# In a fused attention and feed-forward kernel: a cast of g moved from VectorE to ScalarE in batch index 1, sums of the weight forms put behind g's remainder, P's blocks in pairs

## The chip, the cores and the metric

The kernel runs on one core of one Trainium2 chip. The metric is the device time of one execution in microseconds, given as the median of several runs. Five units matter here: PE (TensorE, which runs the matmuls), ACT (ScalarE), DVE (VectorE), and the queues of SP (SyncE) with the DMA engines behind it, which load and store. PE, DVE and ACT each take their instructions strictly in the order in which the program has them, so an instruction that waits holds up whatever stands behind it on its engine.

## The reference: what is computed

Attention through 32 memories a head, then a feed-forward layer. Eight batch indices b, 8 heads, 576 positions, head size 64; model width 512, inner width 2048. Cut to what matters:

```python
a = softmax(phi, axis=2)                    # over the 576 positions
k_m = einsum('bhsm,bhsd->bhmd', a, k)       # 32 memories a head
v_m = einsum('bhsm,bhsd->bhmd', a, v)
scores = matmul(q, k_m.T) / 8
attn = softmax(scores, axis=-1)             # over the 32 memories
x = matmul(attn, v_m)                       # laid out as (4608, 512)
h = x @ w_in                                # (512, 2048)
g = h * sigmoid(h)
out = g @ w_out                             # (2048, 512)
```

All in float32. The matmuls get there by splitting an operand into a high part of fewer bits and the remainder, each in the type fp32r, and adding up three products (high x high, high x low, low x high).

## The kernel before

**The fold.** x is never formed. For each batch index the kernel makes P = v_m x w_in on PE (`p_mm`, matmuls at L646, in blocks of 512 columns called P(b,0) to P(b,3)), splits it into high and low parts (`pm`: an ACT copy at L674, a DVE subtraction at L676), and the first feed-forward product is then h = attn x P, 256 memories deep instead of 512.

**Slots.** The main loop runs over b = 0..7 and, in each, over 16 slots. In a slot of b = 0 or 1, PE makes one block of h (L698, 12 matmuls of 128x288 into the PSUM bank pair `h`), ACT takes SiLU of the 512 main tokens into `gbuf` (L725) and of the 64 tokens left over into `gleft` (L727), and `split` makes g's high part ghi (L715, a DVE cast) and its remainder glo = g - ghi (L717, DVE). PE then runs the second product of the slot *before* it (`acc`, L743, 12 matmuls of 128x512, of which every third reads glo). So in PE's queue a slot reads: h(s), then the events of the slot, then acc(s-1). There is one `h` buffer: h(s+1) starts when L725 and L727 of slot s have read h. From b = 2 on, the second product has another shape (L851 for h, L865 to L881 for g's parts, L890 for 21 matmuls of `sum`), in the manner of Strassen, with fewer multiplications; it needs sums and differences of blocks of w_out, the *forms*. After the 16 slots of an odd b come four *left steps*, in which the tokens left over of two batch indices go through the second product (`accleft`, L743 in b = 1; `lsum`, L974, in b = 3, 5, 7).

**The forms** are prepared once, in the slots of b = 1, by `w_forms(j, step)`, j = 0..7. Step 0 is on DVE: a sum of w_out's high and low parts (L811, 128x1024), then four additions of 128x256 (L815 to L818). Step 1 splits the four results into high parts (L832, on ACT, `t` and `kept`) and remainders (L833, DVE). For even j both steps stand in one slot (2, 5, 8, 11), for odd j step 1 follows one slot after step 0.

**The next batch's attention** is spread over the slots in small steps, which a table of events sets: `ev(b, slot, function, ...)`. They are the maximum of phi (`phi_max`), its folding over the partitions (`phi_fold`), the subtraction, the exponential (`phi_exp`, L319 on ACT, in slot 3 of b = 1), the product with k and v (`e_mm`, L335, slot 5), the turning of its result (`e_tr`, L367 on PE and L368/L369 behind it, slot 9), the scores (`s_all`, L382, slot 10), their softmax (`s_max` L426, `s_sub` L430, `s_exp` L434, `s_sum` L438, `s_norm` L444), turned back as attn's parts, and P's blocks. Exponential and SiLU need different tables of ACT's, so `phi_exp` and `s_exp` each stand between two table loads.

**What sets the order.** PE's order is that of the code. ACT's is too, from b = 1 on. On DVE and SP the framework sorts the instructions by its own estimates, unless `behind(i, other)` adds an edge, so that i is placed after other. `run` and the loop of b = 1 call the functions; `last_split` holds the instructions that made g's remainders so far. e_tr, s_all and e_mm write their results into columns of the `h` banks that L698 leaves free, and wait for L727 (L867 from b = 2 on) of the same slot, which reads there.

## Time and profile before

| | |
|---|---|
| median of 3 runs | 678.95 us (678.32 to 679.55) |
| the profiled execution | 678.81 us, of which its span 677.0 us |
| PE, share of the span busy | 99% |
| DVE | 77% |
| ACT | 55% |
| b = 1, from 106.54 to 197.58 us | 91.04 us: PE 90.94, DVE 76.13, ACT 39.48 us busy |
| b = 2, from 197.58 to 268.95 us | 71.37 us: PE 71.06, DVE 54.23, ACT 39.46 us busy |

A row of the timeline has the start in us, the duration in us, the engine, the line, the operation, what it writes and reads, the shape and how many instructions the row holds; in brackets the idle time ahead of it and who ended it. PE's matmuls are pipelined, so the modelled durations of neighbours overlap: the distance from start to start is what a step costs PE. A regular slot of b = 1 shows as the distance from one h row to the next.

### The profile page before, as it was taken

To read this page: it belongs to the slowest core of one execution; us is meant where nothing else is said; L and a number is where in the kernel's file an instruction comes from. 1 tells how busy PE (TensorE), PEld (TensorE's weight loads), DVE (VectorE), ACT (ScalarE), POOL (GpSimd) and SP (SyncE) were. 2 spreads that over 40 slices of the span, in tenths; PEclk is the share of its full clock that TensorE was granted. 3 is DMA by queue.
4 is the path that set the end of the run, shared out by engine and by line. 5 is a ranking of instruction groups with operands and counts; after the bars stand their busy time and mean duration, and the time that the engine had idled before them with its cause. 6 is when DMAs were issued, how large, how long until landed. Compare 5 with 4: busy or idle time off the path is not lost.

```text
span 677.0 us, 14546 instructions
## 1 busy us (share of the span) xinstructions
PE 667.3 (99%) x5794; PEld 588.6 (87%) x5794; DVE 518.2 (77%) x1092; ACT 369.1 (55%) x682; POOL 0.7 (0%) x6
## 2 busy tenths in 40 slices
PE   8999999999999999999999999999999999999997
PEld 3578778787888998999988999899997999889996
DVE  4897899888948689868877678877877668867653
ACT  3878684533625556654655546564654546554541
POOL 0000000000000000000000000000000000000000
PEclk9999999999999999999999999999999999999999
DMA  9988984224270552253520535216430304300001
GB/s 338 374 321 295 307 312 174 93 106 147 80 233 21 185 176 106 79 189 111 178 98 16 185 95 178 72 40 239 156 127 32 86 2 156 106 35 17 32 1 47
DMA packets 37907, 93.92 MB, mean 139 GB/s; under 512 B 4688, under 2 KB 21456, under 8 KB 34256
## 3 DMA queue, kind: packets, MB, share of 16 engines
q1 hardware_dynamic: 36816, 90.22, 38.5%
q10 hardware_dynamic: 1024, 2.77, 1.1%
q8 instruction: 46, 0.75, 0.5%
q14 instruction: 21, 0.17, 0.1%
HBM read 77.22 MB, written 15.73 MB: 137 GB/s over the span
## 4 chain that ended last, share of the span: by engine, by line
PE 85%; DVE 4%; ACT 2%; issue 2%; DMA 1%; SPq 0%; DVEq 0%; ACTq 0%
PE sum L890 34%; PE h L851 21%; PE acc L743 10%; PE h L698 5%; PE lsum L974 5%; PE bg L646 4%; PE accleft L743 2%; DMA q<-in_q 1%; PE bg L335 1%; PE h L335 1%; PE bg L382 1%; PE pacc L646 1%; ACT raw L174 0%; ACT aparts L879 0%; DVE win L178 0%
## 5 line engine op out<-in xcount | busy, mean ns | idle before, releaser
L851 PE MATMUL h<-aparts,pm 128*128 128x288 f32 x1152 | 168.7, 295 | 0.0
L851 PEld LDWEIGHTS h<-aparts,pm 128*128 128x128 f32 x1152 | 157.4, 188 | 0.8
L865 ACT ACTIVATE gbuf<-h 128x512 f32<-128x512 f32 x96 | 57.3, 597 | 117.0 <-PE h L851 113.7
L890 PE MATMUL sum<-wo_hi,aparts 128*128 128x256 f32 x384 | 102.6, 289 | 0.0
L890 PE MATMUL sum<-kept,aparts 128*128 128x256 f32 x576 | 100.1, 282 | 0.0
L890 PE MATMUL sum<-wo_lo,aparts 128*128 128x256 f32 x384 | 100.0, 282 | 0.0
L870 DVE TENSOR_TENSOR gbuf<-gbuf 128x256 f32<-128x256 f32 x96 | 40.6, 423 | 71.4 <-ACT gbuf L865 70.9
L879 ACT ACTIVATE aparts<-gbuf 128x512 fp32r<-128x512 f32 x86 | 54.4, 633 | 63.5 <-DVE gbuf L874 63.5
L743 PE MATMUL acc<-wo_hi,gparts 128*128 128x512 f32 x256 | 85.0, 397 | 0.1
L890 PEld LDWEIGHTS sum<-wo_hi,aparts 128*128 128x128 f32 x384 | 72.7, 189 | 11.5 <-ACT gleft L867 10.1
L890 PEld LDWEIGHTS sum<-kept,aparts 128*128 128x128 f32 x576 | 82.6, 191 | 0.0
L881 DVE TENSOR_TENSOR gparts<-gbuf,aparts 128x512 fp32r<-128x512 f32 x86 | 59.6, 693 | 19.6 <-ACT aparts L879 19.6
L890 PE MATMUL sum<-wo_hi,gparts 128*128 128x256 f32 x384 | 73.2, 281 | 0.0
L890 PEld LDWEIGHTS sum<-wo_lo,aparts 128*128 128x128 f32 x384 | 73.1, 190 | 0.0
L890 PE MATMUL sum<-kept,gparts 128*128 128x256 f32 x288 | 65.5, 282 | 0.0
L743 PEld LDWEIGHTS acc<-wo_hi,gparts 128*128 128x128 f32 x256 | 47.6, 188 | 14.0 <-DVE t L833 1.7
L890 PEld LDWEIGHTS sum<-wo_hi,gparts 128*128 128x128 f32 x384 | 59.4, 190 | 0.0
L698 PEld LDWEIGHTS h<-aparts,pm 128*128 128x128 f32 x372 | 51.8, 188 | 6.3 <-issue 2.3
L698 PE MATMUL h<-aparts,pm 128*128 128x288 f32 x372 | 56.0, 299 | 0.4 <-ACT aparts L611 0.4
L869 ACT ACTIVATE aparts<-gbuf 128x384 fp32r<-128x384 f32 x96 | 50.4, 525 | 0.0
L743 PE MATMUL acc<-wo_lo,gparts 128*128 128x512 f32 x128 | 49.4, 393 | 0.3 <-DVE wo_lo L182 0.2
L890 PEld LDWEIGHTS sum<-kept,gparts 128*128 128x128 f32 x288 | 47.9, 190 | 0.0
(225 smaller groups left out, 955.9 us busy)
## 6 DMA issues: line engine op xcount, KB each, us to landing
win<-win_saved SPq DMA_DIRECT2D x24, 1024.0 KB, 4.9
kv<-in_kv SPq DMA_DIRECT2D x28, 516.0 KB, 4.9
q<-in_q SPq DMA_DIRECT2D x16, 576.0 KB, 6.3
raw<-in_w_in SPq DMA_DIRECT2D x14, 512.0 KB, 7.3
raw<-in_w_out SPq DMA_DIRECT2D x6, 1024.0 KB, 7.2
win_saved<-win SPq DMA_DIRECT2D x4, 1024.0 KB, 8.6
phi<-in_phi SPq DMA_DIRECT2D x7, 576.0 KB, 8.4
out<-oo SPq DMA_DIRECT2D x26, 128.0 KB, 2.1
```

Of the source, the lines that this page charges most:

```text
L335: nc.tensor.matmul(pt[p][M * r : M * (r + 1), :KVW], e[:, p, c, M * r : M * (r + 1)], kvt[c][:, p, r], start=c == 0, stop=False, skip_grou ...
L646: nc.tensor.matmul((bg[p][M * r : M * (r + 1)] if beside else bg[M * r : M * (r + 1), p, :w]).rearrange("p (k f) -> p k f", f=P), kvT[D * ...
L698: nc.tensor.matmul(h[:, hf, :HALF], wt[:, p, fs], a[:, p, hf * HALF : (hf + 1) * HALF], start=n[hf] == 0, stop=n[hf] == 5, skip_group_chec ...
L743: nc.tensor.matmul(acc[key], gt[:, cs], wt[:, fc], start=fc == 0 and n == 0, stop=fc == NFC - 1 and n == 2)
L851: nc.tensor.matmul(h[:, i, :HALF], wt[:, p, f : f + P], a[:, p], start=n == 0, stop=n == 5)
L865: nc.scalar.activation(gbuf[:, :MAIN].rearrange("p (i f) -> p i f", i=2), h[:, :, :w], AF.Silu)
L869: nc.scalar.activation(hi[:, :3], g[:, 1:4], AF.Copy)
L870: nc.vector.tensor_tensor(g[:, 4:6], g[:, :1].broadcast_to([P, 2, P]), g[:, 1:3], op=ALU.subtract)
L879: nc.scalar.activation(hi[:, 3:], g[:, 4:], AF.Copy)
L881: last_split.append(nc.vector.tensor_tensor(lo[:, 3:], g[:, 4:], hi[:, 3:], op=ALU.subtract))
L890: nc.tensor.matmul(sums[bank][:, place * Q : (place + 1) * Q], gt[:, k], wt, start=bank not in begun, stop=True, skip_group_check=True,)
L974: nc.tensor.matmul(sums[k], part[gt][:, 2 * i + k], wt[:, fc], start=n == 0 and i == 0 and m == 0, stop=True, skip_group_check=True,)
```

## The change

- **g's high part.** In b = 1 (and in the last slot of b = 0) ghi is made by an ACT copy (L713), which comes right behind L727 in ACT's queue, and not by the DVE cast L715.
- **The forms' first sum.** L811 of every j is now placed behind g's remainder (L717) of the slot in which it is called; before, this held for j = 0 alone.
- **P's blocks two by two.** P(2,0) and P(2,1) stood in slots 12 and 14 of b = 1, each alone; now both stand at the third left step of b = 1, interleaved, the second one in a free pair of `acc` banks. P(2,2) and P(2,3) stood in slots 1 and 2 of b = 2; now both stand in slot 0. P(3,0) and P(3,1) go from slots 13 and 14 of b = 2 to 12 and 14. The last quarter of the saved w_in that P(2,3) needs is loaded at the first left step of b = 1, where it was loaded in slot 0 of b = 2.
- **The attention steps of b = 2.** e_tr goes from slot 8 to 7, s_all from 9 to 8, s_max from 10 to 9. The maximum of phi for batch index 4 goes in halves, in slots 10 and 13; it was whole in slot 14.

Lines behind L811 have a number smaller by one in the changed kernel (L832 is L831, L833 is L832 there).

```diff
             i = nc.vector.tensor_tensor(f, as_f32(wo_hi[:, c]), as_f32(wo_lo[:, c]), op=ALU.add)
-            if j == 0:
-                behind(i.ins, last_split[-1])
+            behind(i.ins, last_split[-1])
...
-        ev(b, ex + 4, e_tr, n)
-        ev(b, ex + 5, s_all, n)
-        ev(b, 9 if early else 10, s_max, n, ALL)
+        ev(b, ex + 4 - (not early), e_tr, n)
+        ev(b, ex + 5 - (not early), s_all, n)
+        ev(b, 9, s_max, n, ALL)
...
-            ev(b, NFC + 2 if b % 2 else 13 + k, p_mm, n, k * JW, JW, True, b % 2 and k)
+            ev(b, NFC + 2 if b % 2 else (13 if early else 12 + k) + k, p_mm, n, k * JW, JW, True, b % 2 and k)
...
-            ev(b, 7 if early else 14, phi_max, m)
+            for p in range(2):
+                ev(b, 7 if early else 10 + 3 * p, phi_max, m, (0, 1) if early else (p,))
+                if early:
+                    break
...
-            pair = b > 2 and b % 2 == 0
+            pair = b % 2 == 0
             if not pair:
                 ev(b, 0, win_load, b, 3)
-            ev(b, 0 if b > 2 else 1, p_mm, b, 2 * JW, JW)
+            ev(b, 0, p_mm, b, 2 * JW, JW)
...
-            for k in range(3):
-                ev(b, 12 if k == 2 else 6 + k, win_load, n, k)
+            for k, slot in enumerate((6, 7, 12, NFC)):
+                ev(b, slot, win_load, n, k)
             for k in range(2):
-                ev(b, 12 + 2 * k, p_mm, n, k * JW, JW)
+                ev(b, NFC + 2, p_mm, n, k * JW, JW, True, k)
...
-            gs = split(silu(b, fc, h))
+            gs = split(silu(b, fc, h), steps=(2, 1) if b or fc == NFC - 1 else (0, 1))
...
-                if b > 1:
-                    run(b, NFC + n)
+                run(b, NFC + n)
```

**DVE, slots 8 and 9 of b = 1.** `wf` is the workspace of one j of the forms (j = 4 here, then j = 5 from the last row of before), `gparts` holds ghi and glo, `t_1605` and `kept` take the forms' parts, kvT is e_tr's result. Before:

```order
L811 TENSOR_TENSOR wf<-wo_hi,wo_lo 128x1024
L815 TENSOR_TENSOR wf<-wf 128x256
L816 TENSOR_TENSOR wf<-wf 128x256
L715 CAST gparts<-gbuf 128x512
L817 TENSOR_TENSOR wf<-wf 128x256
L717 TENSOR_TENSOR gparts<-gbuf,gparts 128x512
L818 TENSOR_TENSOR wf<-wf 128x256
L833 TENSOR_TENSOR t_1605<-wf,t_1605 128x256
L833 TENSOR_TENSOR kept<-wf,kept 128x2x256
L833 TENSOR_TENSOR kept<-wf,kept 128x256
L811 TENSOR_TENSOR wf<-wo_hi,wo_lo 128x1024
```

The same place of the changed kernel:

```order
L717 TENSOR_TENSOR gparts<-gbuf,gparts 128x512
L811 TENSOR_TENSOR wf<-wo_hi,wo_lo 128x1024
L814 TENSOR_TENSOR wf<-wf 128x256
L815 TENSOR_TENSOR wf<-wf 128x256
L832 TENSOR_TENSOR t_1605<-wf,t_1605 128x256
L816 TENSOR_TENSOR wf<-wf 128x256
L817 TENSOR_TENSOR wf<-wf 128x256
L832 TENSOR_TENSOR kept<-wf,kept 128x2x256
L832 TENSOR_TENSOR kept<-wf,kept 128x256
L368 COPY kvT_1654<-h 128x128
L717 TENSOR_TENSOR gparts<-gbuf,gparts 128x512
```

Slot 8's remainder (L717) stood behind the sum L811 and three of the four additions; now it stands ahead of all five, and the cast L715 is gone. The next slot's remainder now stands behind e_tr's copy L368, where the next sum L811 stood ahead of that copy and of the remainder.

**ACT, slots 11 to 13 of b = 1.** `t_1776` and `kept` are the forms' high parts of j = 6, `gbuf` and `gleft` the SiLUs of slots 12 and 13, `sc` the scores, of which L434 takes the exponential, `pm<-bg` the high part of P(2,0). Before:

```order
L832 ACTIVATE t_1776<-wf 128x256
L832 ACTIVATE kept<-wf 128x2x256
L832 ACTIVATE kept<-wf 128x256
L725 ACTIVATE gbuf<-h 128x512
L727 ACTIVATE gleft<-h 128x64
L434 ACT_TABLE_LOAD
L434 ACTIVATE sc_1703<-sc_1703 128x1152
L674 ACTIVATE pm<-bg 128x1024
L725 ACT_TABLE_LOAD
L725 ACTIVATE gbuf<-h 128x512
L727 ACTIVATE gleft<-h 128x64
```

The same place of the changed kernel:

```order
L831 ACTIVATE t_1776<-wf 128x256
L831 ACTIVATE kept<-wf 128x2x256
L831 ACTIVATE kept<-wf 128x256
L725 ACTIVATE gbuf<-h 128x512
L727 ACTIVATE gleft<-h 128x64
L713 ACTIVATE gparts<-gbuf 128x512
L434 ACT_TABLE_LOAD
L434 ACTIVATE sc_1703<-sc_1703 128x1152
L725 ACT_TABLE_LOAD
L725 ACTIVATE gbuf<-h 128x512
L727 ACTIVATE gleft<-h 128x64
```

The copy of g's high part L713 has come between slot 12's SiLU and the table load for the exponential, and the copy of P(2,0) has left its place ahead of the load back.

## The prediction

> **What bounds the kernel now.** The page comes first, its row of busy shares:

> ```profile
> PE 667.3 (99%) x5794; PEld 588.6 (87%) x5794; DVE 518.2 (77%) x1092; ACT 369.1 (55%) x682; POOL 0.7 (0%) x6
> ```

> PE is busy for 667.3 us of the span of 677.0, so only two things can move the time: what PE itself has to do, and the few places where it waits. A gain must be PE work left out or one of those waits ended; a loss is a new wait. The windows by batch index show where there is room beside PE (columns: length, then busy us of PE, PEld, DVE, ACT):

> ```profile
> 106.54:197.58 91.04, 90.94 (x644) 73.92 (x642) 76.13 (x149) 39.48 (x75) 0.00 (x0) 1.00 0.41 144
> ```

> In b = 1, where the change is, DVE is busy 84% and ACT 43% of the stage. That is a mean; PE waits or not by what stands in one queue at one moment. So I went on to the timeline of each engine, slot by slot. PE's, in b = 1:

> ```profile
> 125.21 1.76 PE L698 MATMUL h<-aparts,pm 128*128 128x288 f32 x12
> ...
> 127.53 0.73 PE L743 MATMUL acc<-wo_hi,gparts 128*128 128x512 f32 x2
> ...
> 129.94 1.75 PE L698 MATMUL h<-aparts,pm 128*128 128x288 f32 x12
> ...
> 153.59 0.44 PE L367 MATMUL h<-ident,kvn 128*128 128x128 f32 x2
> ...
> 158.31 1.09 PE L382 MATMUL bg<-q,kvT 64*32 64x288 f32 x32
> 159.24 0.35 PE L382 MATMUL h<-q,kvT 64*32 64x64 f32 x16
> ...
> 162.38 1.75 PE L698 MATMUL h<-aparts,pm 128*128 128x288 f32 x12
> ...
> 166.71 1.75 PE L698 MATMUL h<-aparts,pm 128*128 128x288 f32 x12
> ...
> 172.28 1.75 PE L698 MATMUL h<-aparts,pm 128*128 128x288 f32 x12
> ...
> 176.61 1.75 PE L698 MATMUL h<-aparts,pm 128*128 128x288 f32 x12
> ```

> From h row to h row an undisturbed slot takes 166.71 - 162.38 = 4.33 us. The slot with P(2,0) in it takes 172.28 - 166.71 = 5.57, so one block of P alone costs 1.24. The slot that begins at 125.21 takes 4.73, which is 0.40 too long.

> **The change part by part: gains.** First the pairs. The chain of waits has the four left steps of b = 1 without and of b = 3 with a pair of P's blocks:

> ```profile
> 189.57 8.17 PE accleft L743 x36
> ...
> 347.81 2.75 PE lsum L974 x12
> ...
> 352.43 5.67 PE lsum L974 x24
> ```

> 36 matmuls of a left step take 8.17 us; with a pair between them they reach from 347.81 to 352.43 + 5.67 = 358.10, which is 10.29. A pair costs 2.12, two blocks apart 2 x 1.24 = 2.48: a gain of 0.36. There are two new pairs (left step of b = 1, slot 0 of b = 2), and I price both by this row: **-0.72**.

> Second, the wait behind 125.21. On DVE:

> ```profile
> 125.66 1.22 DVE L811 TENSOR_TENSOR wf<-wo_hi,wo_lo 128x1024 f32<-128x1024 f32 x1
> 126.80 0.68 DVE L717 TENSOR_TENSOR gparts<-gbuf,gparts 128x512 fp32r<-128x512 f32 x1
> ...
> 137.38 0.35 DVE L361 TENSOR_SCALAR kvn<-h,rs 128x128 f32<-128x128 f32 x1 [0.43 <-ACT kvn L359]
> ...
> 147.05 1.22 DVE L811 TENSOR_TENSOR wf<-wo_hi,wo_lo 128x1024 f32<-128x1024 f32 x1
> ...
> 167.21 1.35 DVE L430 TENSOR_TENSOR sc<-sc,smx 128x1152 f32<-128x1152 f32 x1
> ```

> The forms' sum went ahead of the slot's remainder, which ended at 127.48; PE's matmul that reads it began at 127.53. With the sum behind the remainder this goes: **-0.40**.

> Third, b = 2, in PE's timeline:

> ```profile
> 241.47 1.09 PE L382 MATMUL bg<-q,kvT 64*32 64x288 f32 x32
> 242.75 0.35 PE L382 MATMUL h<-q,kvT 64*32 64x64 f32 x16 [0.18 <-ACT gleft L867]
> ...
> 249.72 1.76 PE L851 MATMUL h<-aparts,pm 128*128 128x288 f32 x12
> ...
> 253.83 1.76 PE L851 MATMUL h<-aparts,pm 128*128 128x288 f32 x12
> ...
> 258.05 1.87 PE L851 MATMUL h<-aparts,pm 128*128 128x288 f32 x12
> ...
> 263.47 1.76 PE L851 MATMUL h<-aparts,pm 128*128 128x288 f32 x12
> ...
> 268.98 1.77 PE L851 MATMUL h<-aparts,pm 128*128 128x288 f32 x12
> ```

> The second part of s_all comes 1.28 after the first here, and 159.24 - 158.31 = 0.93 in b = 1: 0.35 of waiting for gleft. The slots from 253.83 take 4.22, 5.42 and 5.51, against 4.11 ahead of them and 4.11 + 1.24 = 5.35 with a block: 0.11 + 0.07 + 0.16 = 0.34. All of these steps are respaced; I take both waits to go, **-0.69** (0 to -0.69, since respaced steps can meet other ones). Gains in all: 0.72 + 0.40 + 0.69 = **1.81**.

> **Losses.** They come from ACT's queue, which in b = 1 keeps the order of the code. ACT's timeline, and the group that prices the new copy:

> ```profile
> 118.33 0.60 ACT L725 ACTIVATE gbuf<-h 128x512 f32<-128x512 f32 x1 [3.45 <-PE h L698]
> ...
> 124.32 0.58 ACT L725 ACTIVATE gbuf<-h 128x512 f32<-128x512 f32 x1
> ...
> 128.81 0.60 ACT L725 ACTIVATE gbuf<-h 128x512 f32<-128x512 f32 x1
> 129.30 0.22 ACT L727 ACTIVATE gleft<-h 128x64 f32<-128x64 f32 x1
> ...
> 148.39 0.60 ACT L725 ACTIVATE gbuf<-h 128x512 f32<-128x512 f32 x1 [2.57 <-issue]
> ...
> 152.67 0.60 ACT L725 ACTIVATE gbuf<-h 128x512 f32<-128x512 f32 x1 [0.90 <-PE h L698]
> ...
> 164.22 0.60 ACT L725 ACTIVATE gbuf<-h 128x512 f32<-128x512 f32 x1 [3.90 <-PE h L698]
> ...
> 170.25 0.21 ACT L727 ACTIVATE gleft<-h 128x64 f32<-128x64 f32 x1
> 170.48 1.28 ACT L434 ACT_TABLE_LOAD   x1
> ...
> 175.40 0.60 ACT L725 ACTIVATE gbuf<-h 128x512 f32<-128x512 f32 x1
> ```

> ```profile
> L879 ACT ACTIVATE aparts<-gbuf 128x512 fp32r<-128x512 f32 x86 | 54.4, 633 | 63.5 <-DVE gbuf L874 63.5
> ```

> The same copy, 128x512 to fp32r, takes 0.63 us here. Back to back I count 0.55, since a SiLU of 0.60 is followed 0.49 later (128.81 to 129.30). A SiLU and its small one take 0.49 + 0.22 = 0.71. In most slots ACT waits for h and the copy is free. It isn't free where ACT's queue runs without a gap into the next SiLU; there are three such places.

> *Slots 3 to 5.* The window over this one slot shows ACT full, 4.69 of 4.73 us:

> ```profile
> 125.21:129.94 4.73, 4.63 (x25) 3.77 (x25) 4.38 (x10) 4.69 (x7) 0.00 (x0) 1.00 0.00 0
> ```

> It holds table load, exponential, load and the SiLU of slot 4 without a gap. Put in ahead of the first load, the copy moves that SiLU to 129.36 and its end to 130.07. h of slot 5 could start at 125.21 + 4.33 = 129.54. **+0.55**, which takes back the 0.40 just gained. Then h of slot 6 waits for L361 (at 137.38), which reads e_mm's result out of h and now has more of the forms ahead of it on DVE: between 0 and 0.4, I take **+0.2**.

> *Slot 9.* The sum of j = 4 ran at 147.05, in DVE's gap ahead of slot 8's split. Now it waits for the remainder, which waits for the copy, which waits for the SiLU at 148.39. Behind it come four additions, then `kept` on ACT, and `kept` stands ahead of slot 9's SiLU. How long that chain is shows where a sum already stood behind its split (j = 0, slot 2): 124.32 - 118.33 = 5.99 from SiLU to SiLU. The copy on ACT, longer than the cast, adds 0.1, so slot 9's SiLU comes at 148.39 + 6.09 = 154.48 in place of 152.67, and both SiLUs end at 155.19. The e_tr of slot 9 follows that in PE's queue and waits for it; it ran at 153.59. **+1.6** (1.0 if `kept` finds a gap, 2.2 if DVE is late besides). All of PE's later work queues behind it.

> *Slots 11 to 13* (times as before, since this whole stretch shifts together). j = 6 has the same chain: from slot 11's SiLU at 164.22 to slot 12's 6.09, and 0.3 more as s_sub (1.35, at 167.21) now stands ahead of the remainder and is not quite hidden: 170.6, end 171.3. h of slot 13 could start at 166.71 + 4.33 = 171.04 now that P(2,0) is gone: 0.3. Then copy, load, exponential, load: from the load at 170.48 to the SiLU at 175.40 it took 4.92, of which about 1.25 belonged to P(2,0)'s copy and its wait. So slot 13's SiLU comes at 171.3 + 0.55 + 3.67 = 175.5, its end at 176.25, and h of slot 14 then. Without waits it would be 171.04 + 4.33 = 175.37: **+0.9** in all (0 to 1.2). Put otherwise: the P block that left this slot leaves a hole, and ACT fills it.

> [...]

> The rest I price at nothing, the loads too:

> ```profile
> win<-win_saved SPq DMA_DIRECT2D x24, 1024.0 KB, 4.9
> ```

> A quarter of w_in lands 4.9 us after its issue. The last one is issued at the first left step now, and the left steps take 8.17 + 2.12 until slot 0 of b = 2 needs it; if it were late by the rest of its time, PE would wait there for about that rest. If the first half of phi's maximum, at slot 10 of b = 2, had to wait for its workspace, the DVE work queued behind it would be late, and PE for that; the third rival prices it.

> Losses: 0.55 + 0.2 + 1.6 + 0.9 = **3.25**. Net 3.25 - 1.81 = +1.44, on the profiled execution's 678.81: 680.25, said as **680.2**. That execution lies 0.14 under the median of the runs, so the basis needs no correction.

> **The rivals.**

> *ACT has room, and only the gains stay.* The windows speak for it: ACT 39.48 of 91.04, DVE 76.13; taking sixteen casts off the fuller engine should shorten the chains that end in `kept`, and slot 2, where the sum stood behind the split before, cost PE nothing. It decides if slot 9's SiLU still ends ahead of 153.59, and slots 4 and 13 likewise: then all four losses vanish, 678.81 - 1.81 = **677.0**. Against it: the chain of 6 us was measured, with a slot of 4.33. [...]

> *Half of it.* Slot 9 and slot 4 lose as worked out, but slots 6 and 11 to 13 catch up, since PE's longer wait at slot 9 also lets DVE clear its queue: 0.55 + 1.6 - 1.81 = +0.34, **679.1**.

> *DVE blocks in b = 2.* The half maximum at slot 10 waits for its workspace, and the respaced steps meet others: the 0.69 is not gained, three slots more come late by 0.16 each as the one at 263.47 does (0.5), and h of slot 6 takes the upper 0.4: 1.44 + 0.69 + 0.5 + 0.2 = +2.83, **681.6**.

> That the change does not do what it says is ruled out by the order of the instructions, which shows each move.

> **How the numbers follow.** A difference of 0.2%, 1.36 us, is about what a measurement of this kernel can tell from no change. My forecast (+1.44) gets 0.50; with its terms' bounds it is above 1.36 in somewhat over half of that, 0.30, and within in 0.20. Half of it: 0.24 (0.20 within, 0.03 slower, 0.01 faster). Only gains: 0.15 (0.12 faster, 0.03 within). Blocked b = 2: 0.11, slower. Together faster 0.13, same 0.43, slower 0.44. The range leaves out the most of the rival with gains alone and a tail above: from 678.2, half a microsecond and more under the 679.1 of the halfway case, to 681.8, above the worst case's 681.6.

> **What the changed profile would show.** Slot 9 of b = 1: SiLU (L725) about 6.1 after slot 8's, L367 with PE idle over 1 us ahead of it and gleft L727 as the releaser. Slots 3 to 5: h rows 4.9 apart, not 4.33. Slots 12 to 14: two h rows that are 4.6 and 5.0 apart. The left steps of b = 1 longer by 2.1, slots 12 and 14 without L646. In b = 2, 0.9 between the two rows of s_all. It is wrong if L367 follows L646 without a gap, or if PE's idle time in b = 1 does not grow.

## The result, and the profile after

The changed kernel takes **684.07 us** (median of 6 runs, 682.77 to 685.5), the kernel before 678.74 (6 runs, 678.32 to 679.55): ratio 1.0076, 95% interval 1.0065 to 1.0087. It is slower, by 5.3 us. The direction was forecast; the size was forecast as 1.4, and the time lies outside the range of 678.2 to 681.8.

The page of the changed kernel, busy shares and the row of the granted clock in 40 slices:

```profile
PE 668.4 (98%) x5794; PEld 590.0 (86%) x5794; DVE 513.3 (75%) x1079; ACT 378.0 (55%) x701; POOL 0.7 (0%) x6
PEclk9999999999999999899999999999999999999999
```

PE's busy time grew by 1.1 us only, the span by 5.3: most of the loss is waiting. And one slice, the seventeenth (from 273 to 290 us), has a clock below full, which the profiled execution of the kernel before does not have anywhere. First PE's timeline in b = 1, where the prediction put its losses:

```profile
105.84 1.85 PE L698 MATMUL h<-aparts,pm 128*128 128x288 f32 x12
...
124.52 1.80 PE L698 MATMUL h<-aparts,pm 128*128 128x288 f32 x12
...
129.51 1.85 PE L698 MATMUL h<-aparts,pm 128*128 128x288 f32 x12 [0.46 <-ACT gleft L727]
...
137.89 1.86 PE L698 MATMUL h<-aparts,pm 128*128 128x288 f32 x12 [0.28 <-DVE kvn L361]
...
155.36 0.44 PE L367 MATMUL h<-ident,kvn 128*128 128x128 f32 x2 [1.60 <-ACT gleft L727]
...
168.41 1.75 PE L698 MATMUL h<-aparts,pm 128*128 128x288 f32 x12
173.24 1.87 PE L698 MATMUL h<-aparts,pm 128*128 128x288 f32 x12 [0.34 <-ACT gleft L727]
178.29 1.86 PE L698 MATMUL h<-aparts,pm 128*128 128x288 f32 x12 [0.44 <-ACT gleft L727]
182.73 1.75 PE L698 MATMUL h<-aparts,pm 128*128 128x288 f32 x12
```

Every new wait in b = 1 stands where it was forecast, with the releaser that was forecast: the h rows of slots 5, 6, 13 and 14, and L367 in slot 9. ACT's timeline has the two chains behind them:

```profile
124.32 0.64 ACT L713 ACTIVATE gparts<-gbuf 128x512 fp32r<-128x512 f32 x1
124.97 1.28 ACT L319 ACT_TABLE_LOAD   x1
...
148.45 0.60 ACT L725 ACTIVATE gbuf<-h 128x512 f32<-128x512 f32 x1 [2.03 <-PE h L698]
...
154.62 0.58 ACT L725 ACTIVATE gbuf<-h 128x512 f32<-128x512 f32 x1
```

The copy stands ahead of the table load and takes 0.65 from start to start there; from slot 8's SiLU to slot 9's it is 6.17, where 6.09 was worked out. In b = 2 the steps run without the waits of before:

```profile
239.48 1.09 PE L382 MATMUL bg<-q,kvT 64*32 64x288 f32 x32
240.41 0.35 PE L382 MATMUL h<-q,kvT 64*32 64x64 f32 x16
...
255.59 1.76 PE L850 MATMUL h<-aparts,pm 128*128 128x288 f32 x12
...
260.91 1.76 PE L850 MATMUL h<-aparts,pm 128*128 128x288 f32 x12
...
265.00 1.76 PE L850 MATMUL h<-aparts,pm 128*128 128x288 f32 x12
...
270.31 1.77 PE L850 MATMUL h<-aparts,pm 128*128 128x288 f32 x12
```

The two parts of s_all are 0.93 apart, and slots 12 to 14 take 5.32, 4.09 and 5.31. At the last slot of b = 2 the changed kernel is 270.31 - 268.98 = 1.33 us late. That this is close to the forecast of 1.44 is partly luck. In this execution b = 1 began at 105.84, 0.70 earlier than the 106.54 of before; the prediction has no term ahead of b = 1, and the 0.70 is there already at the h row of 86.36 (before 87.06), up to which both kernels run the same instructions. Counted from the start of b = 1, the loss up to here is 2.03. The other 4 us are lost in the next few microseconds, at a place of which the prediction does not speak: slot 1 of b = 3. PE there, in the changed kernel, with the window behind the wait (length, busy us of PE, PEld, DVE, ACT, POOL, then the granted clock):

```profile
279.73 1.75 PE L850 MATMUL h<-aparts,pm 128*128 128x288 f32 x12
...
284.15 0.39 PE L889 MATMUL sum<-wo_hi,aparts 128*128 128x256 f32 x1 [1.97 <-DVE x L930]
...
287.36 2.27 PE L850 MATMUL h<-aparts,pm 128*128 128x288 f32 x12
```

```profile
284.10:289.40 5.30, 5.20 (x27) 5.00 (x28) 4.52 (x11) 0.63 (x1) 0.00 (x0) 0.68 0.15 49
```

```profile
285.08:288.50 3.42, 3.42 (x16) 3.42 (x17) 3.13 (x8) 0.63 (x1) 0.00 (x0) 0.50 0.23 77
```

From h row to h row it is 7.63 us. PE waits 1.97 for L930, which reads the sums of b = 2 out of PSUM. The 0.68 of the window of 5.30 us is a mean: for 3.42 us of it the granted clock is 0.50, ahead of that and behind it 1.00. In the kernel before the same slot takes 4.07:

```profile
278.40 1.75 PE L851 MATMUL h<-aparts,pm 128*128 128x288 f32 x12
...
282.47 1.74 PE L851 MATMUL h<-aparts,pm 128*128 128x288 f32 x12
```

Why L930 came late, DVE's timeline and SP's queue show. Before:

```profile
279.34 0.41 DVE L931 TENSOR_TENSOR x<-sum,oo 128x256 f32<-128x256 f32 x1
...
281.11 0.29 DVE L303 COPY wide<-fm 128x256 f32<-128x256 f32 x1
```

```profile
270.78 0.32 SPq L88 DMA_DIRECT2D win<-win_saved  x1
272.51 2.48 SPq L88 DMA_DIRECT2D qz<-qm  x4
278.12 1.82 SPq L88 DMA_DIRECT2D fm<-fm  x3
```

After:

```profile
282.81 0.29 DVE L303 COPY wide<-fm 128x256 f32<-128x256 f32 x1 [1.73 <-DMA fm<-fm]
283.02 0.42 DVE L930 TENSOR_TENSOR x<-sum,oo 128x256 f32<-128x256 f32 x1
```

```profile
273.32 2.48 SPq L88 DMA_DIRECT2D qz<-qm  x4
275.90 0.53 SPq L88 DMA_DIRECT2D win<-win_saved  x1
277.29 1.77 SPq L88 DMA_DIRECT2D fm<-fm  x3
```

Two orders have turned round. On DVE, L303 (the last step of folding phi's maximum for batch index 4, which waits for the small moves `fm`) now stands *ahead* of L930, and PE waits for L930. On SP, the 1 MB load of w_in's last quarter now stands *between* the fold's two moves. The DMA issues of the stretch from 270 to 290 us give the landing time of the second move, changed kernel first, then before:

```profile
fm<-fm SPq DMA_DIRECT2D x3, 1.0 KB, 4.7
```

```profile
fm<-fm SPq DMA_DIRECT2D x3, 1.0 KB, 1.8
```

A move of 1 KB issued behind a load of 1 MB took 4.7 us in place of 1.8. Why the move takes longer behind the load, no run shows.

### The profile page after: what moved, and what is told of

The parts are those of the page before. It is cut to its first block, busy times and chain, and to the rows that moved or that the text cites. A ratio compares the mean times of both kernels' runs of the same rounds, so it can differ in the third digit from the quotient of the medians.

```text
span 682.3 us, 14535 instructions
## 1 busy us (share of the span) xinstructions
PE 668.4 (98%) x5794; PEld 590.0 (86%) x5794; DVE 513.3 (75%) x1079; ACT 378.0 (55%) x701; POOL 0.7 (0%) x6
## 4 chain that ended last, share of the span: by engine, by line
PE 79%; DVE 7%; ACT 5%; issue 2%; DMA 1%; SPq 0%; DVEq 0%; ACTq 0%
PE sum L889 32%; PE h L850 20%; PE acc L743 8%; PE h L698 5%; PE lsum L973 5%; PE bg L646 3%; PE accleft L743 2%; PE bg L335 1%; PE bg L382 1%; PE pacc L646 1%; ACT gbuf L725 1%; DVE wf L811 1%; DMA fm<-fm 1%; DMA kv<-in_kv 1%; PE h L335 1%
## 5 line engine op out<-in xcount | busy, mean ns | idle before, releaser
L878 ACT ACTIVATE aparts<-gbuf 128x512 fp32r<-128x512 f32 x86 | 54.4, 633 | 64.2 <-DVE gbuf L873 64.2
L743 PE MATMUL acc<-wo_hi,gparts 128*128 128x512 f32 x256 | 84.3, 394 | 0.0
L698 PEld LDWEIGHTS h<-aparts,pm 128*128 128x128 f32 x372 | 51.5, 188 | 9.3 <-ACT gleft L727 3.4
L698 PE MATMUL h<-aparts,pm 128*128 128x288 f32 x372 | 56.5, 300 | 1.9 <-ACT gleft L727 1.2
L743 PEld LDWEIGHTS acc<-wo_hi,gparts 128*128 128x128 f32 x256 | 47.8, 188 | 11.4 <-issue 1.0
L743 PE MATMUL acc<-wo_lo,gparts 128*128 128x512 f32 x128 | 49.4, 393 | 0.3 <-DVE wo_lo L182 0.2
## 6 DMA issues: line engine op xcount, KB each, us to landing
win<-win_saved SPq DMA_DIRECT2D x24, 1024.0 KB, 4.9
raw<-in_w_out SPq DMA_DIRECT2D x6, 1024.0 KB, 7.2
win_saved<-win SPq DMA_DIRECT2D x4, 1024.0 KB, 8.9
```

Source lines behind the costliest of these rows:

```text
L698: nc.tensor.matmul(h[:, hf, :HALF], wt[:, p, fs], a[:, p, hf * HALF : (hf + 1) * HALF], start=n[hf] == 0, stop=n[hf] == 5, skip_group_chec ...
L743: nc.tensor.matmul(acc[key], gt[:, cs], wt[:, fc], start=fc == 0 and n == 0, stop=fc == NFC - 1 and n == 2)
L878: nc.scalar.activation(hi[:, 3:], g[:, 4:], AF.Copy)
```

## The experiments

The main theory after the result: the maximum of phi in halves turned both orders round; DVE's queue passes the late move on to PE; PE's idle time makes the granted clock fall; the rest of the change costs about what was forecast. The first four kernels test this, the next four split the loss in b = 1, the last three look at what is left. All were timed beside the kernel before on the same chip, which took 678.67 to 678.72 us there.

**e1_whole: the maximum whole again.**

```diff
-            for p in range(2):
-                ev(b, 7 if early else 10 + 3 * p, phi_max, m, (0, 1) if early else (p,))
-                if early:
-                    break
+            ev(b, 7 if early else 14, phi_max, m)
```

> The changed kernel with the maximum of phi for batch index 4 whole in slot 14 of b = 2 again; all else as changed. Main theory: the halves were what put the load of w_in's last quarter between the two small moves of the fold, and L303 ahead of L930 on DVE; so PE's wait of 1.97 us in slot 1 of b = 3 goes, the granted clock stays at 1.00 there, and the time is 684.1 - 3.9 = about 680.1 us, which is what the prediction gave for the rest of the change. Rival (the halves have nothing to do with it, the clock fell for a reason of its own): 683 us or more.

680.48 us, ratio 1.0026 (1.0015 to 1.0036). DVE, and the window of the wait:

```profile
281.13 0.41 DVE L930 TENSOR_TENSOR x<-sum,oo 128x256 f32<-128x256 f32 x1
...
282.85 0.29 DVE L303 COPY wide<-fm 128x256 f32<-128x256 f32 x1
```

```profile
281.00:284.10 3.10, 3.10 (x28) 3.10 (x27) 2.94 (x10) 1.16 (x3) 0.00 (x0) 1.00 0.27 81
```

L930 is ahead of L303 again, PE is busy throughout, the clock is 1.00. 3.6 of the 5.3 us come from this one edit.

**e2_fold_late: the halves stay, L303 goes behind L930.**

```diff
-                ev(*((b, 11 + i) if early else (b + i // 2, (14, 15, 0)[i])), phi_fold, m, i, load)
+                ev(*((b, 11 + i) if early else (b + i // 2, (14, 15, 1)[i])), phi_fold, m, i, load)
```

> The changed kernel with the last step of the fold (L303, L304) called one slot later, so that L303 stands behind L930 on DVE; the load of w_in still stands between the fold's two moves. Main theory (the queue on DVE passes the late move on to PE): the move still takes over 4 us, L303 still waits, PE does not; 680.1 us. Rival (the late move costs by itself, through the subtraction from phi and the exponential behind it): PE waits elsewhere in b = 3 and the time stays at 682 us or more.

680.84 us, ratio 1.0034 (1.0021 to 1.0046). On DVE:

```profile
281.11 0.41 DVE L930 TENSOR_TENSOR x<-sum,oo 128x256 f32<-128x256 f32 x1
...
285.07 0.29 DVE L303 COPY wide<-fm 128x256 f32<-128x256 f32 x1
```

The load still stands between the moves, issued at 276.01 with the second move 1.39 us behind it, as far apart as in the changed kernel (275.90 and 277.29), where `fm` took 4.7 us to land. But the move no longer holds up L930, which stands ahead of L303 now. Little is left of the loss: 0.36 us in the median against e1_whole, whose seven runs all lie under these five. In the profiles the difference lies in slots 1 and 3 of b = 3, which take 4.40 and 4.35, in e1_whole 4.07 and 4.09.

**e4_fold_first: the load ahead of both moves, L303 kept ahead of L930.** e1_whole, and:

```diff
-        add(c12, sums[2][:, :Q], c11)
+        i = add(c12, sums[2][:, :Q], c11)
+        if b == 2 and t == 1:
+            behind(i.ins, at[4]["wide"])
```

> As e1_whole (load of w_in ahead of both moves of the fold), but with an edge that keeps L303 ahead of L930 on DVE. If DVE's order alone does it: L303 waits for the end of a chain of moves that is as short as before, until about 282.3, PE waits about 1.2 us, less than the 1.60 that left the clock at 1.00 in slot 9 of b = 1, so 680.1 + 1.2 = 681.3 us. If only the load between the moves does it: 680.1 us. If the place of L303 is all there is to it, and the load nothing: 684 us.

683.90 us, ratio 1.0076 (1.0063 to 1.0088), as slow as the changed kernel. DVE, PE and the window behind the wait:

```profile
282.45 0.29 DVE L303 COPY wide<-fm 128x256 f32<-128x256 f32 x1 [1.75 <-DMA fm<-fm]
```

```profile
283.79 0.39 PE L889 MATMUL sum<-wo_hi,aparts 128*128 128x256 f32 x1 [1.67 <-DVE x L930]
```

```profile
284.10:289.40 5.30, 5.05 (x28) 4.84 (x27) 3.97 (x10) 0.63 (x1) 0.00 (x0) 0.68 0.15 49
```

So L303's place on DVE can cause the whole loss without the load between the moves. It does not follow that the load is harmless in the changed kernel. Here the maximum is whole, and the second move is issued at 279.39, where the changed kernel issues it at 277.29, so that a move which lands in 1.8 us comes as late as one of 4.7 there. With the 3.06 us that e4 takes from that issue to L303, the changed kernel without the load in between would have the move landed at about 280.4, ahead of the 281.13 at which L930 runs in e1_whole. By this estimate both orders are needed for its loss; no run has the halves, L303 ahead and a quick move. My middle figure, 681.3, was wrong twice: the wait was 1.67, not 1.2, and the clock fell although 1.60 in slot 9 of b = 1 had left it alone. It seems to have fallen in some executions only: the five have a mean clock of 0.997, 0.997, 1.000, 0.996 and 0.999, and the two highest belong to the two shortest times, 683.07 and 683.27.

**e3_fill_wait: PE kept busy during the wait.** The changed kernel, with slot 1's h of b = 3 made twice:

```diff
-        for i in range(2):
+        for i in (0, 1, 0, 1) if (b, t, j) == (3, 0, 1) else range(2):
```

> The changed kernel with the 12 matmuls of h in slot 1 of b = 3 done twice (1.6 us of work for PE, same result), so that PE is busy for most of the time in which it waited. Main theory (PE's idle time makes the clock fall): PE still cannot go on before 284.15, but is idle for 0.4 us only, the granted clock stays 1.00, and the time falls by the 1.9 us that the slow matmuls cost: 682.2 us. Rival (the clock falls for another reason): clock 0.68 again, 684 us or more.

682.91 us, ratio 1.0063 (1.0049 to 1.0077). PE, and the window behind the wait:

```profile
279.98 3.33 PE L850 MATMUL h<-aparts,pm 128*128 128x288 f32 x24
```

```profile
284.10:289.40 5.30, 4.93 (x38) 4.73 (x39) 4.92 (x13) 2.03 (x5) 0.00 (x0) 1.00 0.15 49
```

With 12 matmuls *more* the kernel is 1.2 us faster than the changed one, and the clock stays at 1.00; the mean clock of all five executions is 0.999 or 1.000, where the changed kernel has 0.996 or 0.997 in five of six. The sixth, at 0.999, took 682.77, about as long as this kernel. So in this place it is the idle time of PE (1.97 us there, 0.41 here) that makes the clock fall, and the fall costs 1.2 to 1.3 us of the whole time. (The forecast of 1.9 was too high: PE's rows at the lower clock are 1.64 longer, and PE goes on 0.28 later here, at 284.43.)

**e5_cast_back and e6_sums_free: the two halves of the edit in b = 1.** Both are e1_whole; e5_cast_back has the cast on DVE, e6_sums_free has the sums free except for j = 0:

```diff
-            gs = split(silu(b, fc, h), steps=(2, 1) if b or fc == NFC - 1 else (0, 1))
+            gs = split(silu(b, fc, h), steps=(0, 1))
```

```diff
-            behind(i.ins, last_split[-1])
+            if j == 0:
+                behind(i.ins, last_split[-1])
```

> e1_whole with the cast of g's high part back on DVE (L715); the forms' sums stay behind the remainder. e1_whole took 680.5 us. If the moved sums are what makes slot 9 late, as the prediction has it (SiLU to SiLU 5.99 with the cast on DVE, 6.09 with the copy on ACT), L367 in slot 9 still waits about 1.5 us; the price of ACT's copy in slots 3 to 5 (0.55) and its part in slots 12 to 14 (0.5) go: 679.4 us. Rival (the copy on ACT makes slot 9 late, the sums do not): the wait of L367 goes, 677.8 us.

681.45 us, ratio 1.0036 (1.0022 to 1.0051): slower than e1_whole, not faster. L367 waits 1.57 in slot 9 as expected, but a new wait stands ahead of the left steps:

```profile
187.84 0.50 PE L743 MATMUL acc<-wo_hi,gparts 128*128 128x512 f32 x1 [0.67 <-DVE gparts L715]
...
188.78 0.73 PE L743 MATMUL acc<-wo_hi,gparts 128*128 128x512 f32 x2 [0.20 <-DVE gparts L717]
```

With the sums late, DVE's queue reaches the last slot's cast (L715) late, and PE waits for it. The copy on ACT spares that: in the changed kernel no L743 between 182.73 and 200.05 waits.

> e1_whole with the forms' sums free again but for j = 0; g's high part stays on ACT. If the moved sums are the cause: the wait of L367 in slot 9 (1.6) goes, slots 11 to 13 keep part of theirs, slot 4 has the copy's 0.55: 678.7 us. Rival (the copy on ACT is the cause): 680.5 us, with L367 waiting as before.

678.22 us, ratio 0.9990 (0.9981 to 0.9998). PE's e_tr in slot 9:

```profile
153.69 0.44 PE L367 MATMUL h<-ident,kvn 128*128 128x128 f32 x2
```

No wait. The sums behind the remainder make slot 9 late, and the copy does not.

**e7_only_pairs, e8_two_behind.** e7_only_pairs has both edits above; e8_two_behind writes `if j < 2:` in the second.

> e1_whole with both undone: the cast on DVE and the sums free but for j = 0. What is left of the change is P's blocks in pairs and the respaced steps of b = 2. By the prediction's terms (0.72 and 0.69): 678.7 - 1.4 = 677.3 us. Rival (the pairs are worth nothing, since PE's work is the same): 678.0 us or more.

678.07 us, ratio 0.9987 (0.9977 to 0.9997).

> e7_only_pairs with the sums of j = 0 and j = 1 behind the remainder, where before has only j = 0. The wait of 0.40 for the remainder in slot 4 goes without the copy on ACT: 676.9 us. Rival (the sum of j = 1, started later, makes the SiLU of slot 5 late through kept, as j = 4 does in slot 9): 677.3 us or more.

678.09 us, ratio 0.9989 (0.9980 to 0.9997): no difference from e7_only_pairs. Its slot 4 is 0.36 shorter and its slot 5 0.36 longer: the earlier remainder lets PE go on sooner, but L361, for which the h of slot 6 waits, comes 12.17 us after the h row of slot 4 in both.

**e10_pairs_alone: the kernel before, and of the change only the pairs and the load that goes with them.**

```diff
-            pair = b > 2 and b % 2 == 0
+            pair = b % 2 == 0
...
-            ev(b, 0 if b > 2 else 1, p_mm, b, 2 * JW, JW)
+            ev(b, 0, p_mm, b, 2 * JW, JW)
...
-                ev(b, 12 + 2 * k, p_mm, n, k * JW, JW)
+                ev(b, NFC + 2, p_mm, n, k * JW, JW, True, k)
```

> The kernel before with P's blocks of b = 1 and of the first two quarters' partners in b = 2 in pairs, and nothing else of the change. The prediction priced the two pairs at 0.72: 678.7 - 0.7 = 678.0 us. Less what slot 14 of b = 1 hides (the wait of 0.98 seen in e7_only_pairs lay behind P(2,1) before): 678.7 us, if that wait is to be counted against the pairs.

678.72 us, ratio 1.0000 (0.9991 to 1.0009). PE in slots 13 to 15 of b = 1:

```profile
175.33 1.75 PE L698 MATMUL h<-aparts,pm 128*128 128x288 f32 x12
...
177.31 0.50 PE L743 MATMUL acc<-wo_hi,gparts 128*128 128x512 f32 x1 [0.23 <-DVE gparts L715]
...
178.24 0.73 PE L743 MATMUL acc<-wo_hi,gparts 128*128 128x512 f32 x2 [0.20 <-DVE gparts L717]
...
180.64 1.75 PE L698 MATMUL h<-aparts,pm 128*128 128x288 f32 x12
```

The slot whose P block has gone takes 5.31, not 4.33: DVE has its cast and remainder ready only 1 us later. Before, P(2,1) filled that wait. So 1.24 us of work were moved out of this slot and 0.26 were gained there. In the changed kernel, with the copy on ACT, the same slot takes 182.73 - 178.29 = 4.44, and this wait does not arise.

**e11_halves_alone: the kernel before, and of the change only the halves** (the lines that e1_whole takes out).

> The kernel before with the maximum of phi for batch index 4 in halves, in slots 10 and 13 of b = 2, and nothing else of the change. Main theory: L303 gets ahead of L931 on DVE and the load of w_in between the fold's moves; PE waits about 2 us in slot 1 of b = 3, the granted clock falls to about 0.7 for some 5 us: 678.7 + 3.5 = 682.2 us. Rival (it takes the lateness of the other parts of the change): 678.7 us.

680.86 us, ratio 1.0029 (1.0018 to 1.0040). PE in slot 1 of b = 3, and the window behind it:

```profile
282.53 0.39 PE L890 MATMUL sum<-wo_hi,aparts 128*128 128x256 f32 x1 [1.61 <-DVE x L931]
```

```profile
284.10:289.40 5.30, 5.30 (x45) 5.30 (x44) 4.72 (x12) 3.49 (x6) 0.00 (x0) 1.00 0.08 27
```

The same wait arises from this edit alone, 1.61 us, and costs 2.1. The clock stayed at 1.00, against what I expected.

**e9_late_copy: e7_only_pairs, with the copy on ACT in slots 13 to 15 alone.**

```diff
-            gs = split(silu(b, fc, h), steps=(0, 1))
+            gs = split(silu(b, fc, h), steps=(2, 1) if b and fc > 12 else (0, 1))
```

> e7_only_pairs with the copy of g's high part on ACT in slots 13 to 15 of b = 1 alone. In e7_only_pairs PE waited there 0.98 us between the h rows of slots 14 and 15, for the cast and the remainder on a full DVE. If DVE's queue is the cause, a copy on ACT at these slots, behind both table loads, ends it: 678.1 - 0.9 = 677.2 us. Rival (ACT's conversions for the forms stand in the way there too, as in e6_sums_free, where slots 13 and 14 lost 0.57 and 0.42): 678 us or more.

677.95 us, ratio 0.9991 (0.9983 to 1.0000). The slot of 5.31 took 4.65, the stretch behind it 17.75 in place of 17.39: half of the gain is given back at the left steps, and the rest is too small to be told from e7_only_pairs. Four versions (e6 to e9) lie within 0.3 us of each other and 0.5 to 0.8 us under the kernel before; none is better than that.

## Why the prediction was wrong, point by point

**The step that failed** is "The rest I price at nothing, the loads too", with the sentence on the first half of phi's maximum. I asked of the halves only whether their workspace was free, and of the loads only whether a quarter of w_in landed in time for b = 2. What I did not follow is where the moved steps' *successors* went: the fold's moves on SP, past the next batch index's load, and L303 on DVE, past the sums that PE waits for, both in b = 3, behind the stretch that the diff names. e1_whole and e11_halves_alone show that the halves do it, e2_fold_late and e4_fold_first that it reaches PE through DVE's order. Whether that order would cost anything in the changed kernel without the load between the moves, no run shows. Size: 3.6 us of the 5.3 (684.07 against 680.48).

**A second effect in the same place**: PE's wait was 1.97, and the loss 4.1 (slots 1 and 2 of b = 3 took 7.63 + 4.60, before 4.07 + 4.07). By the distances from row to row, 2.45 of the 4.1 are the wait and a short one right behind it, and 1.64 the stretch at the lower clock. e3_fill_wait shows that the clock hangs on PE's idle time here: with 0.41 us of it the window has 1.00, with 1.97 it has 0.68. The prediction had no term for the clock.

**The forecast without that place** was +1.44; e1_whole, which lacks it, measured 680.48 against 678.67, +1.8. Term by term, from the rows of the changed kernel where no other is named:

| term | forecast | measured |
|---|---|---|
| slot 4 (0.40 gained, 0.55 lost) | +0.15 | 129.51 - 124.52 = 4.99, before 4.73: +0.26 |
| slot 5, h of slot 6 behind L361 | +0.2 | 137.89 - 129.51 = 8.38, before 137.78 - 129.94 = 7.84: +0.54 |
| slot 9, L367 | +1.6 | 1.60 |
| slots 12 and 13 | +0.9 | 4.83 + 5.05 against 2 x 4.33: +1.22 |
| two pairs | -0.72 | from slot 15 of b = 1 to slot 2 of b = 2: 31.88, before 30.32; less the 2 x 1.24 gone from slots 12 and 14: -0.92 |
| b = 2 respaced | -0.69 | e7_only_pairs against e10_pairs_alone: -0.65 |
| sum | +1.44 | +2.05; from the first h row of b = 1 to the last of b = 2: +2.03 |

Slot 9 and the respacing were right in mechanism and size. Slots 4, 5, 12 and 13 had the right mechanism and were sized too low, slot 5 by most in proportion. The pairs' term held in the changed kernel, but it does not hold by itself: e10_pairs_alone, with the cast still on DVE, gained 0.0. The pair itself costs what the row of b = 3 said (the left steps of b = 1 take 200.05 - 189.78 = 10.27, before 197.58 - 189.40 = 8.18, so 2.09 for the 2.12 of that row), but the price of a single block, 1.24, is not what a slot gains when the block leaves. In slot 14 a wait on DVE lay hidden behind it, which the copy on ACT takes away in the changed kernel. The prediction did not foresee that tie between the two edits.

**Which edit costs what in b = 1** I had partly wrong. The four kernels with the maximum whole make a square:

| | sums free | sums behind the remainder |
|---|---|---|
| cast on DVE | 678.07 | 681.45 |
| copy on ACT | 678.22 | 680.48 |

The sums cost 3.4 or 2.3. The copy, to which I gave 0.55 and half of slots 12 to 14, costs 0.15 with the sums free, which can't be told from nothing, and *gains* 1.0 with the sums late, since it takes a cast off the full DVE ahead of the left steps. The first rival's argument, that casts taken off the fuller engine shorten the chains, holds in that column of the square (the sums behind the remainder) and not in the other.

**The rivals.** "DVE blocks in b = 2" came nearest in kind (DVE's queue held by an instruction that waits, because of the half maximum), but the instruction is another, it waits for a move and not for its workspace, it stands in b = 3, and the price was 681.6 for 684.1. "Only the gains" and "half of it" are refuted by the 1.60 at L367 and by slots 12 and 13.

**What stays open.** Which idle time lowers the clock. In the profiled executions 1.60 (slot 9 of b = 1) and 1.61 (e11_halves_alone) did not, 1.67 (e4_fold_first) and 1.97 did. The length of the longest piece does not settle it, since by the mean clocks it fell in only some executions of e4_fold_first and in five of six of the changed kernel, and in none of the seven of e11_halves_alone. A second short wait right behind the first does not separate them either: the profile of e11_halves_alone has it too, of the same length as in the changed kernel (0.32 and 0.33 us from start to start, where 0.12 is usual). What differs from one execution to the next, no run shows.

## What to carry to other kernels

Where a step is moved and a scheduler sets the order on other queues, follow the step's successors to their end, and compare the order on every queue in the stretch *behind* the edit too: what cost most here was an instruction that waits for a transfer and has got ahead of one for which the bounding engine waits. The time that a piece of work takes is what a slot gains by losing it only if nothing else in that slot ends later: in e10_pairs_alone 0.26 us were gained for 1.24. And a wait on TensorE can cost well over its length, if the clock falls behind it: here 1.64 us came on top of 2.45.
